# Two steps of the first batch set ahead of a filler, and the filler cut from 22 to 8 identity products

## The chip, the core and the metric

The kernel runs on one core of a Trainium2 chip. A core has a matrix engine (PE in the profile, with PEld for its weight loads), a vector engine (DVE), a scalar engine (ACT), GpSimd (POOL) and SyncE (SP), which here only issues DMAs. Every engine takes its instructions in the order in which they were written down for it, and waits on semaphores for what other engines or DMAs have to deliver. The metric is the time of one execution in microseconds (us) on the device; lower is better. Queries, keys, values and all products are 32-bit floats; the three weight matrices are given in 64 bits.

## What is computed

Retention in its parallel form (8 batches of 576 tokens, 8 heads of 64), followed by a gated feed-forward block on 4608 tokens of width 512, with 1536 hidden columns:

```python
scores = scale * np.matmul(q, k.transpose(0, 1, 3, 2))
gamma = 1.0 - 2.0 ** (-5.0 - np.arange(H, dtype=np.float32))
Dmat = np.where(rel >= 0, gamma[:, None, None] ** rel[None, :, :], 0.0)
attn_out = np.matmul(scores * Dmat[None], v)
x = np.ascontiguousarray(attn_out.transpose(0, 2, 1, 3)).reshape(B * S, H * D)
g = x @ w_gate
out = (g * (1.0 / (1.0 + np.exp(-g))) * (x @ w_val)) @ w_out
```

## The kernel before

**Retention.** Two heads make a pair; a batch has four pairs (0 to 3 in the first batch), and a sequence is cut into chunks of 64 tokens. For each pair the kernel makes transposed queries and keys, the scores of each chunk with itself (`scores`, L558), the sums of keys times values of each chunk (`new_states`, L528), their running, decayed sums over the chunks (`masked`: L565 masks the scores, L569 copies, L581 joins pairs of chunks, L588 runs over odd chunks, L593 fills the even ones), and two contributions to the output: that of the chunk itself (`own_values`, L517), and that of all past chunks, which multiplies the running sums by the queries (`earlier_values`, L544). Before the latter PE waits until the last product of `own_values` is complete. `to_x` (L625) copies the result to `xs`, the input of the feed-forward block.

**Feed-forward.** The first 512 tokens are handled chunk by chunk of the width (a chunk is a pair's 128 columns): `up0(f, chunks, parts)` multiplies the f-th block of 128 hidden columns, part 0 being the gate and part 1 the value weights, each into a bank of its own (bankA and bankB for even f, bankC and bankE for odd f). After the fourth chunk ACT takes the silu (L874) and DVE the product (L875). The other tokens follow in four tiles of 1024, in a scheme with fewer products than the plain one (L1204 and L1410), which fills the time from about 170 us on.

**Weights** arrive as 64-bit floating-point numbers and are rounded to 32 bits on the core before use. `split(j)` is two ACT instructions (L398, L399) that take a half of a loaded weight apart into two buffers, which alternate with j; `rounding(j)` is two DVE instructions (L415, L416) that put the rounded weight together. `split` may also issue the next weight's load, on SP's queue or, from the sixth weight on, on POOL's (L379, L381). SP's queue carries the loads of the pairs too (L269, L273, L279 in the first batch; L290 and L299 later). Pairs of the later batches have their queries and keys transposed by DVE (L477), which then waits for the DMA.

**Order.** The schedule is written out by hand: the order of calls in the function's body is the order on each engine. `pieces` is a list of postponed DVE and ACT work: `go_on(n)` issues the next n of them, and a piece that is itself a list (here L581; L588; L593) can be issued part by part with `part_on()`. The stretch that the change touches runs from about 16 to 22 us of the profile: pair 1's outputs, the first two weights, and the transposes of pair 3 (L466). In it stands a loop of 22 products of a 64x64 corner of the identity with itself into bankB (L1461), whose result nobody reads; PE does them while the first weight is being rounded.

Of the kernel before, what the change touches and what calls it, by code (L numbers as in the profile page):

```python
# [132 lines left out]
def kernel(  # L133
# [110 lines left out]
    def whole(i):  # L244

        return HP <= i < needed(2) - 2
# [136 lines left out]
    def bits_of(i, f):  # L383

        if i < NUP:
            return raws[i].rearrange("p c (f m two) -> p f c m two", f=2, two=2)[:, f]
        return raws[i].rearrange("p (f c) (d m two) -> p f (c d) m two", f=2, m=P, two=2)[:, f]

    def split(j):

        i, f = halves[j]
        bits = bits_of(i, f)
        top, ulp = [rest[:, part_at + 512 * (2 * n + j % 2) : part_at + 512 * (2 * n + j % 2 + 1)] for n in range(2)]
        blocks = lambda a: a.rearrange("p (c m) -> p c m", m=P)
        nc.scalar.activation(out=blocks(top), in_=bits[:, :, :, 1].bitcast(F32), func=AF.Prelu, scale=2.0 ** -112, alpha=2.0 ** 32)  # L398
        nc.scalar.activation(out=blocks(ulp.bitcast(I32)), in_=bits[:, :, :, 0].bitcast(U32), func=AF.Copy, scale=2.0 ** -29)  # L399
        parts[j] = top.bitcast(I32), ulp.bitcast(I32)  # L400
        m = j - 2 if 1 < j < 4 else j // 2
        if f and m != RAWS and m + RAWS + (m < RAWS) < len(order):
            if j == 3:
                held.append(lambda: load_w(m + RAWS + (m < RAWS)))
            else:
                load_w(m + RAWS + (m < RAWS))

    def rounding(j, ahead=True):

        i, f = halves[j]
        dst = weights[i][1][f].bitcast(I32)
        top, ulp = parts.pop(j)
        nc.vector.tensor_scalar(out=dst, in0=top, scalar1=3, scalar2=None, op0=ALU.logical_shift_left)  # L415
        nc.vector.tensor_tensor(out=dst, in0=dst, in1=ulp, op=ALU.add)  # L416
        if ahead and j + 1 < len(halves):
            split(j + 1)
# [23 lines left out]
    def places(i):  # L442
        return other if i < HP and i % 2 else (ret, ret_last, state)
# [56 lines left out]
    def value(i, hl, c):  # L500

        if whole(i):
            x = c // 2 % 2
            at = c % 2 + c // 4 * 2
        else:
            x, at = c % 2, c // 2
        return outer[half[hl ^ x], x, ts(at, L)]

    def own_values(i, n=0):

        s, ret = st[i], places(i)[0]
        cs = [a + d for a in (1 - n, 5 - n) for d in (0, 2)] if whole(i) else range(0 if n else NC - 1)
        for c in cs:
            for hl in range(2):
                rows, at = chunk(i, hl, c)
                start = n == 0 and c in (cs[:2] if whole(i) else (0, 1))
                m = nc.tensor.matmul(value(i, hl, c), s["v"][rows, at], ret[rows, c % 2 if whole(i) else hl, c // 2],  # L517
                                     start=start, stop=start, skip_group_check=True)
        if n == 0:
            s["own"] = m  # L520
# [10 lines left out]
    def earlier_values(i):  # L531
        s, (_, ret_last, state) = st[i], places(i)

        wait = nc.tensor.nop()
        tc.add_manual_dep(wait.ins, s["own"].ins.name,
                          mybir.DependencyInfo(mybir.DependencyClass.Sync, mybir.DependencyReason.DATA), reason="row halves")
        own_values(i, 1)
        for hl in range(0 if i < HP else 2):
            rows, at = chunk(i, hl, NC - 1)
            nc.tensor.matmul(xr[half[hl]], s["v"][rows, at], ret_last[rows],  # L540
                             start=False, stop=False, skip_group_check=True)
        for c in (1, 3, 4, 6, 5, 7, 2, 8) if whole(i) else range(1, NC - (i < HP)):
            for hl in range(2):
                nc.tensor.matmul(xr[half[hl]] if c + 1 == NC else value(i, hl, c), state[half[hl], c, :],  # L544
                                 s["qT"][half[hl], ts(c, L)], start=False, stop=True, skip_group_check=True)
# [52 lines left out]
    def to_x(i):  # L598
        b, p = divmod(i, HP)
        st.pop(i)  # L600

        def blocks(lo, end):
            for n in range(2):
                cs = [c for c in range(lo, end, 2) if c // 2 % 2 == n]
                if not cs:
                    continue
                at = dst(lo, end).rearrange("p (c r i) -> p c r i", r=2, i=L)[:, (cs[0] - lo) // 2 :: 2]
                src = outer[:, n, cs[0] // 4 * P : (cs[-1] // 4 + 1) * P].rearrange("p (c r i) -> p c r i", r=2, i=L)
                for rows, to in exchanged if n else straight:
                    if light(i):  # L610
                        nc.scalar.copy(out=at[to], in_=src[rows])
                    else:
                        decay = (qry_odd if n else qry)[rows, p].unsqueeze(1).unsqueeze(1)
                        nc.vector.tensor_tensor(out=at[to], in0=src[rows], in1=decay.to_broadcast(list(src[rows].shape)), op=ALU.mult)

        def chunks(lo, end):
            for r in range(2):
                cs = range(lo + (lo + r) % 2, end, 2)
                if not cs:
                    continue  # L620
                n = len(cs)
                for src, to in exchanged if r else straight:
                    table = (qry_odd if r else qry)[src, p]
                    if scaled(i):
                        nc.scalar.copy(out=dst(lo, end)[to].rearrange("p (c r i) -> p c r i", r=2, i=L)[:, :, r], in_=xo[src, :, r])  # L625
                        continue
                    at = dst(cs[0] - r, cs[0] - r + 2 * n) if cs[0] - r >= lo and cs[-1] + 2 - r <= end else None
                    if at is not None:
                        at = at[to].rearrange("p (c r i) -> p c r i", r=2, i=L)[:, :, r]
                        nc.vector.tensor_tensor(out=at, in0=xo[src, cs[0] // 2 : cs[0] // 2 + n, r],  # L630
                                                in1=table.unsqueeze(1).to_broadcast([at.shape[0], n, L]), op=ALU.mult)
                    else:
                        for c in cs:
                            nc.vector.tensor_tensor(out=dst(c, c + 1)[to], in0=xo[src, c // 2, r], in1=table, op=ALU.mult)

        def both():

            if i < HP:
                pass
            elif light(i):  # L640
                nc.scalar.copy(out=dst(NC - 1, NC), in_=xr)
            else:
                nc.vector.tensor_tensor(out=dst(NC - 1, NC), in0=xr, in1=qry[:, p], op=ALU.mult)
            lo = 0
            while lo < NC - 1:
                end = lo + 1
                while end < NC - 1 and where(end)[0] == where(lo)[0]:
                    end += 1
                if whole(i):
                    blocks(lo, end)  # L650
                else:
                    chunks(lo, end)
                lo = end

        def dst(lo, end):
            n, o = where(lo)
            return xs[n][:, p, o : o + (end - lo) * L]

        def where(c):

            n, o = divmod(b * S + c * L - starts[0], TW)
            return n, o - (TW - T0 if n == 0 else 0)

        return [both]
# [109 lines left out]
                             start=False, stop=True, skip_group_check=True)  # L774
        nc.scalar.copy(out=xs[0][:, 0], in_=outer[:, 0])

    def new_pair(i):
        scores(i, True)
        new_states(i)
        pieces.extend(masked(i))  # L780
        go_on(3)

    def turn_pair(i):
        for f in transposes(i):
# [54 lines left out]
    def go_on(n):  # L839
        for _ in range(min(n, len(pieces))):  # L840
            while part_on():
                pass

    def part_on():

        if pieces and isinstance(pieces[0], list):
            pieces[0].pop(0)()
            if pieces[0]:
                return True
            pieces.pop(0)  # L850
        elif pieces:
            pieces.pop(0)()
        return False
# [600 lines left out]
    split(0)  # L1454
    rounding(0, False)
    scale_run(3)
    new_pair(2)
    own_values(1)
    split(1)
    for _ in range(22):  # L1460
        nc.tensor.matmul(bankB[0:D, 0:D], ident[0:D, 0:D], ident[0:D, 0:D], start=True, stop=True)  # L1461
    up0(0, [0], [0])
    earlier_values(1)
    to_x(1)[0]()
    put = transposes(3)
    rounding(1, False)
    for f in put:
        f()
    up0(0, [1], [0])
    up0(0, [0], [1])  # L1470
# [161 lines left out]
```

## Time and profile before

| | |
|---|---|
| three runs | 1014.41 us median, 1012.95 to 1018.09 |
| the profiled execution | 1013.87 us |
| its span, first to last instruction | 1012.2 us |
| PE busy | 1005.7 us (99%) |
| DVE, POOL, ACT busy | 713.4, 571.9, 286.4 us |
| PE idle before 1.55 us | start of the first product |
| granted clock of PE | 1.00 |

Times in the profile count from the span's start. A line of a timeline gives the start, the duration from the first to the last instruction of the group, engine, source line, operation, the tile written and those read, the shape, and how often; in brackets stands the engine's idle time before it and what ended it. PE's 32-bit products appear as two records each, so 22 products are x44. A line of the chain of waits gives start, duration and what was being done or waited for. In rows by stretches, each engine has its busy time and its number of records; the last three columns are the granted clock, the share of the 16 DMA engines that was in use (transfers that overlap count each, so it can pass 1), and GB/s.

### The profile page before, as it was taken

The numbers are of one execution on the slowest core, as the hardware profiler recorded it, in microseconds if no ns is written. First come the engines' busy times: TensorE is split into PE (matmuls) and PEld (weight loads), VectorE is DVE, ScalarE is ACT, GpSimd is POOL, SyncE is SP. The second block draws the span as 40 slices with busy tenths as digits, with TensorE's granted clock in tenths as the row PEclk, the third lists the DMA queues.
The fourth block names the chain that finished last, engine by engine and source line by source line (L and its number), as shares of the span: only waits on it lengthen the run. The fifth ranks groups of instructions, "written<-read, shape, count | busy, mean of one in ns | idle before, by whom it ended". The sixth has DMA issues, their size and how long they took to land.

```text
span 1012.2 us, 21328 instructions
## 1 busy us (share of the span) xinstructions
PE 1005.7 (99%) x8338; PEld 829.4 (82%) x8338; DVE 713.4 (70%) x1203; ACT 286.4 (28%) x636; POOL 571.9 (57%) x603
## 2 busy tenths in 40 slices
PE   9999999999999999999999999999999999999998
PEld 7655555888888888888888888888888888888887
DVE  5567988677875766977777678866575767566645
ACT  4644622131423312133322202233320012233110
POOL 3510458979475228575565157746672586566514
PEclk9999999999999999999999999999999999999999
DMA  9999986888788887757668686434454554445553
GB/s 242 280 265 258 201 236 230 222 236 217 182 209 215 215 213 215 195 157 197 180 183 225 176 203 197 152 131 161 162 173 141 154 189 147 146 155 184 179 161 103
DMA packets 273932, 194.44 MB, mean 192 GB/s; under 512 B 212328, under 2 KB 241896, under 8 KB 273832
## 3 DMA queue, kind: packets, MB, share of 16 engines
q1 hardware_dynamic: 248296, 94.77, 38.6%
q10 hardware_dynamic: 21360, 84.29, 25.5%
q0 software_dynamic: 4176, 14.03, 4.3%
q8 instruction: 66, 1.08, 0.5%
q14 instruction: 34, 0.28, 0.1%
HBM read 154.11 MB, written 38.93 MB: 191 GB/s over the span
## 4 chain that ended last, share of the span: by engine, by line
PE 90%; SPq 3%; DVE 2%; DMA 2%; issue 1%; POOL 1%; ACT 1%; ACTq 0%; DVEq 0%; POOLq 0%
PE bankC L1204 11%; PE bankB L1204 11%; PE bankA L1204 11%; PE bankE L1204 11%; PE bankB L1410 7%; PE bankE L1410 7%; PE bankC L1410 7%; PE bankA L1410 6%; SPq L299 2%; PE inner L1204 2%; PE outer L1204 2%; PE outer L517 2%; PE outer L544 1%; PE inner L558 1%; PE inner L528 1%
## 5 line engine op out<-in xcount | busy, mean ns | idle before, releaser
L1060 POOL TENSOR_TENSOR rest<-rest 128x512 f32<-128x512 f32 (+1 forms) x139 | 147.8, 1075 | 159.9 <-DVE rest L1060 112.5
L1219 POOL TENSOR_TENSOR arena<-rest,io 128x256 f32<-128x256 f32 x168 | 123.5, 746 | 89.9 <-ACT io L1218 89.3
L1218 ACT ACTIVATE io<-rest 128x256 f32<-128x256 f32 x192 | 79.2, 417 | 200.8 <-DVE rest L1060 138.9
L1204 PE MATMUL bankB<-rest,arena 128*128 128x256 f32 x448 | 114.9, 380 | 0.1
L1060 DVE TENSOR_TENSOR rest<-bankB,rest 128x512 f32<-128x512 f32 x116 | 78.6, 686 | 41.8 <-PE bankB L1204 30.0
L1204 PE MATMUL bankC<-rest,arena 128*128 128x256 f32 x416 | 106.3, 380 | 0.0
L1204 PE MATMUL bankA<-rest,arena 128*128 128x256 f32 x412 | 104.8, 379 | 0.0
L1060 DVE TENSOR_TENSOR rest<-bankA,rest 128x512 f32<-128x512 f32 x111 | 75.3, 686 | 38.4 <-PE bankA L1204 19.2
L1060 DVE TENSOR_TENSOR rest<-bankC,rest 128x512 f32<-128x512 f32 x110 | 74.6, 685 | 37.6 <-PE bankC L1204 26.6
L1060 DVE TENSOR_TENSOR rest<-bankE,rest 128x512 f32<-128x512 f32 x106 | 71.9, 686 | 36.5 <-PE bankE L1204 21.4
L1204 PE MATMUL bankE<-rest,arena 128*128 128x256 f32 x372 | 94.9, 380 | 0.0
L1204 PEld LDWEIGHTS bankB<-rest,arena 128*128 128x128 f32 x448 | 84.5, 190 | 12.8 <-POOL arena L1060 0.7
L1204 PEld LDWEIGHTS bankC<-rest,arena 128*128 128x128 f32 x416 | 78.5, 190 | 11.4 <-DVE rest L1060 0.8
L1204 PEld LDWEIGHTS bankA<-rest,arena 128*128 128x128 f32 x412 | 78.1, 190 | 10.8
L1204 PEld LDWEIGHTS bankE<-rest,arena 128*128 128x128 f32 x372 | 70.3, 190 | 10.1 <-DVE rest L1060 0.6
L1060 POOL TENSOR_TENSOR arena<-arena 128x256 f32<-128x256 f32 (+1 forms) x76 | 70.4, 950 | 8.1 <-PE bankC L1204 6.7
L1410 PE MATMUL bankB<-arena 128*128 128x256 f32 x264 | 61.0, 381 | 0.0
L1410 PE MATMUL bankE<-arena 128*128 128x256 f32 x264 | 60.8, 380 | 0.0
L1410 PEld LDWEIGHTS bankE<-arena 128*128 128x128 f32 x264 | 50.0, 190 | 6.9
L1410 PEld LDWEIGHTS bankB<-arena 128*128 128x128 f32 x264 | 49.8, 190 | 6.9
L1410 PE MATMUL bankC<-arena 128*128 128x256 f32 x240 | 55.2, 379 | 0.0
L1410 PE MATMUL bankA<-arena 128*128 128x256 f32 x228 | 52.5, 380 | 0.0
(291 smaller groups left out, 1875.3 us busy)
## 6 DMA issues: line engine op xcount, KB each, us to landing
arena<-up ACTq DMA_DIRECT2D x63, 896.0 KB, 4.8
arena<-dn ACTq DMA_DIRECT2D x65, 384.0 KB, 3.1
arena<-dn SPq DMA_DIRECT2D x39, 384.0 KB, 3.1
out_dram<-rest SPq DMA_DIRECT2D x31, 256.0 KB, 4.5
qk<-in_q_dram SPq DMA_DIRECT2D x108, 72.0 KB, 4.4
qk<-in_k_dram SPq DMA_DIRECT2D x108, 72.0 KB, 3.3
dn<-rest SPq DMA_DIRECT2D x26, 256.0 KB, 3.6
up<-arena SPq DMA_DIRECT2D x13, 512.0 KB, 4.8
```

The costliest lines, as they stand in the source:

```text
L299: queue.dma_start(out=qk[a * SQ : (a + 1) * SQ, n], in_=src[b, 2 * p + a // 2, :, (a % 2) * SQ : (a % 2 + 1) * SQ].rearrange("(j t) d -> t ...
L517: m = nc.tensor.matmul(value(i, hl, c), s["v"][rows, at], ret[rows, c % 2 if whole(i) else hl, c // 2], start=start, stop=start, skip_grou ...
L528: nc.tensor.matmul(z[half[hl], r, c], s["kn"][chunk(i, hl, 2 * c + r)], s["v"][rows, at], start=True, stop=True, skip_group_check=True)
L544: nc.tensor.matmul(xr[half[hl]] if c + 1 == NC else value(i, hl, c), state[half[hl], c, :], s["qT"][half[hl], ts(c, L)], start=False, stop ...
L558: nc.tensor.matmul(sc[chunk(i, hl, 2 * c + r)[0], r if whole(i) else hl, c], kT[half[hl], at], qT[half[hl], at], start=True, stop=True, sk ...
L1060: eng.tensor_tensor(out=out, in0=a, in1=b, op=ALU.add if sign > 0 else ALU.subtract)
L1204: m = nc.tensor.matmul(b[:, g * TB : (g + 1) * TB], w[:, g], x, start=(opens and g == 0), stop=True, skip_group_check=True)
L1218: nc.scalar.activation(out=s, in_=src[:, 0:TB], func=AF.Silu)
L1219: (nc.vector if busy and o != 2 and qd + 1 < NQ else nc.gpsimd).tensor_tensor(out=hid[:, qd, 2 * H + h, 2 * T + t], in0=src[:, TB : 2 * TB ...
L1410: nc.tensor.matmul(b[:, m * TB : (m + 1) * TB], lhs[:, qd, ts(m, P)], w[:, qd], start=(opens and qd == 0 and m == 0), stop=(qd == NQ - 1), ...
```

## The change

In the first batch, between the scores of pair 2 and the transposes of pair 3:

- `new_pair(2)` issues two postponed pieces instead of three, and L581 of the third by itself; the rest of it (three L588 and L593, the running sums of pair 2) follows after the second weight's rounding.
- `earlier_values(1)` and `to_x(1)` of pair 1 stand ahead of the identity products and of the first product with a weight, instead of behind.
- `rounding(1)` stands ahead of L588 and L593 on DVE, instead of behind.
- The loop makes 8 identity products instead of 22.

What is computed stays the same. On SP and POOL, and on ACT, the order of instructions is unchanged; on PE the 14 products of L544 change places with the identity products and one L871; on DVE one L415 and one L416 change places with the running sums.

```diff
-    def new_pair(i):
+    def new_pair(i, n=3):
         scores(i, True)
         new_states(i)
         pieces.extend(masked(i))
-        go_on(3)
+        go_on(n)
...
     scale_run(3)
-    new_pair(2)
+    new_pair(2, 2)
+    part_on()
     own_values(1)
+    earlier_values(1)
     split(1)
-    for _ in range(22):
+    rounding(1, False)
+    go_on(1)
+    to_x(1)[0]()
+    for _ in range(8):
         nc.tensor.matmul(bankB[0:D, 0:D], ident[0:D, 0:D], ident[0:D, 0:D], start=True, stop=True)
     up0(0, [0], [0])
-    earlier_values(1)
-    to_x(1)[0]()
-    put = transposes(3)
-    rounding(1, False)
-    for f in put:
+    for f in transposes(3):
         f()
```

## The prediction

> **What bounds the kernel now.** I read the page first. PE is busy 1005.7 of 1012.2 us, and the list of PE's own waits over the whole span holds six entries. So the question is not what the edit saves, but whether PE can use it. The chain of waits shows the place of the edit:
>
> ```profile
> 16.05 0.47 PE outer L517 x32
> 16.52 2.51 PE bankB L1461 x44
> 19.03 1.06 PE bankA L871 x2
> 20.09 0.61 PE outer L544 x28
> 20.70 0.59 PE bankC L466 x4
> ```
>
> The 22 identity products (L1461, two records each) are 44 records in 2.51 us, that is 57 ns a record and 114 ns a product. They stand in the chain because PE's order is fixed, while PE's next real work, L871, needs the first rounded weight: that is DVE's L416 at 17.47 + 0.69 = 18.16, 0.8 us before L871 starts. So at least some of the filler is not needed. The list of PE's waits is the second view:
>
> ```profile
> PE bankB L732 <- POOL ident masks.py:199: 1.6, 1, 1.6
> PE bankA L871 <- ACT io L874: 0.4, 1, 0.4
> PE inner L747 <- DVE kT L741: 0.3, 1, 0.3
> PE bankA L871 <- ACT rest L625: 0.2, 1, 0.2
> ```
>
> The second entry decides my forecast: PE waits once more, 80 us after the edit. Timelines of PE, ACT and DVE around it, in this order:
>
> ```profile
> 102.36 3.70 PE L871 MATMUL bankA<-rest,arena 128*128 128x512 f32 x8 [0.38 <-ACT io L874]
> 98.11 0.68 ACT L398 ACTIVATE rest<-rest 128x512 f32<-128x512 f32 x1 [7.61 <-issue]
> 101.73 0.57 ACT L874 ACTIVATE io<-bankA 128x512 f32<-128x512 f32 x1
> 96.03 0.78 DVE L477 STREAM_TRANSPOSE kT<-qk 128x576 f32<-128x576 f32 x1 [3.45 <-DMA qk<-in_k_dram]
> 97.60 0.43 DVE L415 TENSOR_SCALAR arena<-rest 128x512 int32<-128x512 int32 x1
> ```
>
> Read from the bottom: DVE stands 3.45 us before its transposition L477 until a key block has landed at 96.03. Behind it in DVE's queue is the rounding L415 (to 98.03). ACT's next split L398 needs the buffer that L415 reads, and starts at 98.11 after 7.61 us of idleness. Three splits stand ahead of the silu L874, which frees PE's bank at 102.30. So at 102.36 PE is held by a DMA landing, with 0.38 us to spare. Last, the DMA by stretches (the last two columns are DMA share and GB/s):
>
> ```profile
> 20.00:62.00 42.00, 41.53 (x393) 25.18 (x393) 22.19 (x46) 23.05 (x45) 18.63 (x30) 1.00 1.15 282
> 62.00:102.00 40.00, 39.98 (x400) 20.04 (x398) 32.77 (x72) 22.73 (x41) 5.30 (x7) 1.00 1.02 256
> 102.00:1012.00 910.00, 906.06 (x7236) 768.38 (x7236) 648.20 (x1065) 232.21 (x535) 540.39 (x550) 1.00 0.65 185
> ```
>
> From 20 to 102 us the transfers fill the DMA engines (share 1.15 and 1.02); afterwards 0.65, and PE waits no more.
>
> **The change, part by part.** The sum goes against the profiled execution: 1013.87 us, span 1012.2, so 1.67 around it; the median of the three runs, 1014.41, lies 0.54 above.
>
> *PE up to 22 us.* Removed: 14 products x 0.114 = 1.60 us; the eight left take 0.91. Moved: L544 of pair 1 (0.61) now follows L517, ending at 16.52. It also needs the states of L593 (15.48 + 0.48 = 15.96, done) and L517's completion, which cost 0.09 us at the next such place (24.53 to 24.62): start 16.61, end 17.22, products until 18.13. L871 then waits for L416 (18.16); the shortest releases seen cost 0.05, so 18.21, end 19.27. Next are pair 3's transposes L466. Their key blocks were issued at about 14.7 and 15.2; blocks of L273 landed 3.5 to 4.1 us after issue, the query blocks of L269 5.5, so the second is there between 18.7 and 20.7. I take 19.5, near the key row: PE waits 0.2 to 0.3, L466 starts at 19.55 (20.63 before). The scaled queries (POOL's L720, 18.79 + 1.04 = 19.83) are there for the second four at 20.04. Then L871's second chunk needs ACT's three L625 (1.13): ACT is free at 18.58 + 0.66 = 19.24, L544 ended at 17.22, so 20.37, and PE comes at 20.64. Before: 21.93, with a wait of 0.21 that now goes. **Lead: 21.93 - 20.64 = 1.3 us.** With the late bound of the keys it is 0.1, with the early one 1.5.
>
> *DVE.* The second rounding (L415, L416; 20.86 to 22.11 = 1.25) goes ahead of three L588 and L593 (19.18 to 20.95 = 1.77). Its splits are done at 19.24, so it ends at 19.15 + 1.25 = 20.4; its reader, L871 into bankB, comes at 22.89 - 1.3 = 21.6. The states now end at 22.2; their reader L544 of pair 2 comes at 24.62 - 1.3 = 23.3. So this move costs nothing while 1.1 us of cover is left; if rounding came later than that, PE would lose the excess. Nothing else on DVE is overtaken.
>
> *ACT, POOL, SP.* Their orders are unchanged; instructions only come earlier. The fourth split (L398 at 26.39) needs a weight piece issued at about 19.9; such a piece took 5.4, so 25.3: ACT gains 1.0 instead of 1.3. Its rounding then ends at 27.3 (28.36), before bankE's L871 at 27.9. So PE keeps its 1.3 beyond 30 us. No DMA is added or reordered within a queue. SP's weight load at 24.15 waits for an L399 and comes earlier by up to 1.3, but two loads of 1 MB, issued at 20.48 and 21.02, are in flight; POOL's at 27.94 and 35.18 come 1.0 to 1.3 earlier.
>
> *From 30 to 102 us.* PE has no wait in between, and its suppliers there have margins above a microsecond or move with it. At 102.36 the silu still hangs on the landing at 96.03. From 24.15 on SP issues loads back to back, each as room becomes free, and the engines are full, so I leave 96.03 where it is: the wait grows from 0.38 to 1.68 us and takes back the whole 1.3. Bounds: -1.3 if the landing moves along, +1.3 by the second rival below. I take zero, since DVE's stall of 3.45 is wider than any lead.
>
> Sum: 1013.87 - 1.3 + 1.3 = 1013.9; beside the median, **1014.4 us**.
>
> **A rule beside a row.** PE's transposes of 128x128 take 0.85 us for four at 5.09 (bankE) and 0.45 for four at 6.77 (bankC) in the chain, after steady work since 1.55; the granted clock reads 1.00 throughout. PE starts at half pace and doubles after some 5 us. The Trainium skill, "TensorE: Matmul & The Clock Gate", Part 1, says that the clock is halved until some 3.4 us of sustained work, and halved again after an idle window of that length. The trace agrees with the doubling; none of its idle stretches after 7 us is long enough to show the rest. By that rule the removed filler could cost the pace, and an estimate from the page would be 3.4 us at half rate, 1.7 us lost.
>
> **The rivals.**
> *The lead survives.* If the key blocks land 1.3 us earlier, or PE isn't held at 102 in typical executions, the gain stays: 1014.4 - 1.3 = 1013.1. For it: the margin is only 0.38, and DMA dips to share 0.93 between 15 and 20 us. Against: the share of 1.15 afterwards.
> *Earlier weight loads push the keys back (slower).* POOL's loads are released by ACT, hence by PE. Up to 1.3 us earlier, they use engines that SP's key blocks use. At 282 GB/s, half to POOL, 1 to 1.3 us are 140 to 180 KB, so keys land 0.5 to 0.65 later; if it repeats for the next pair, 1.3. PE then waits longer at 102: +0.5 to +1.3, so 1014.9 to 1015.7, say 1015.2. It decides as soon as the landing moves later at all, because the lead has made PE the waiting side. Against: what POOL takes early it doesn't take later. The Trainium skill, "DMA: Bandwidth & Descriptors", on queues, rings and completion order, has each engine take turns between its queues; this speaks for this case, and no row here shows the turns.
> *PE drops to half pace near 19 us (slower).* At half pace for the 5 us that the start took, PE loses 2.6; less the lead of 1.3 and the margin of 0.38, +0.9: 1015.3. Against: the new idle pieces sum to some 0.4 us, and the present kernel had 0.29 and 0.21 without a change of pace.
> *The change does nothing of what it says:* excluded, the order of instructions on PE and DVE shows both moves.
>
> **How the numbers follow.** Chances: held at 102, no change, 0.60; lead survives 0.18; keys pushed back 0.15; half pace 0.03; something that I don't see 0.04. The runs of before spread from 1012.95 to 1018.09, so medians wobble by about a microsecond. The range takes in 1013.1 and 1015.7 and 0.9 on either side: 1012.2 to 1016.6. A measurement tells about 0.5%, 5 us, from no change. No case has a price near it; only the unseen one could: faster 0.02, same 0.95, slower 0.03.
>
> **What would show it.** Right: L871's second chunk at about 20.6; PE's wait at 102 about 1.7, with L477's landing within 0.5 of 96.0; everything behind shifted by less than 0.5. Lead surviving: that landing near 95, the wait still below 0.5. Keys pushed back: landing after 96.5. Half pace: L871's records doubled around 20 us. Wrong in the first step: L466 waiting beyond 20.2, or L544 of pair 2 waiting for L593.

## The result, and the profile after

The changed kernel takes 1019.83 us (median of 7 runs, 1017.31 to 1022.43) where the kernel before takes 1014.00 (7 runs beside it): a ratio of 1.0050, 95% interval 1.0036 to 1.0065. It is slower by half a per cent, and the interval lies clear of 1. In a second series it was 1017.73 against 1014.02, ratio 1.0035 (1.0016 to 1.0053). The prediction said no change. The profiled execution took 1019.12 us, with a span of 1017.4, 5.2 us longer than before.

Around the edit nearly all of it came as written down. Timeline of PE and DVE of the changed kernel (start, duration, engine, line, operation, tile, shape, count; in brackets idle time and what ended it):

```profile
19.70 0.63 PE L466 MATMUL bankC<-ident,rest 128*128 128x128 f32 x4 [0.19 <-DMA rest<-in_k_dram]
20.61 1.02 PE L871 MATMUL bankA<-rest,arena 128*128 128x512 f32 x2
21.47 1.02 PE L871 MATMUL bankB<-rest,arena 128*128 128x512 f32 x2
23.29 0.68 PE L544 MATMUL outer<-rest,state 64*64 64x64 f32 x28 [0.18 <-PE outer L517]
28.33 1.98 PE L871 MATMUL bankE<-rest,arena 128*128 128x512 f32 x4 [0.29 <-DVE arena L416]
31.73 1.12 PE L871 MATMUL bankA<-rest,arena 128*128 128x512 f32 x2
...
19.21 1.03 DVE L415 TENSOR_SCALAR arena<-rest 128x512 int32<-128x512 int32 x1
20.38 0.69 DVE L416 CUSTOM_DVE_ANT_0 arena<-arena,rest 128x1024 uint16<-128x1024 uint16 x1
```

The second chunk starts at 20.61 (21.93 before): the lead of 1.3 us is there. At 31.73 it has shrunk to 0.77 (32.50 before), because the fourth rounding came later than I had it. Four entries from the list of PE's waits then show what the lead became:

```profile
PE bankA L871 <- ACT io L874: 3.1, 1, 3.1
PE bankA L1204 <- DMA arena<-up: 1.0, 1, 1.0
PE bankE L871 <- DVE arena L416: 0.3, 1, 0.3
PE bankC L1204 <- DMA arena<-up: 0.2, 1, 0.2
```

The first one is eight times the wait that I had looked at, and it is not at 102 us but at 70. Timeline of the changed kernel there:

```profile
67.32 0.78 DVE L477 STREAM_TRANSPOSE kT<-qk 128x576 f32<-128x576 f32 x1 [9.42 <-DMA qk<-in_k_dram]
68.67 0.38 DVE L415 TENSOR_SCALAR arena<-rest 128x512 int32<-128x512 int32 x1
69.14 0.70 ACT L398 ACTIVATE rest<-rest 128x512 f32<-128x512 f32 x1 [12.85 <-DVE arena L415]
72.72 0.58 ACT L874 ACTIVATE io<-bankA 128x512 f32<-128x512 f32 x1
73.35 5.40 PE L871 MATMUL bankA<-rest,arena 128*128 128x512 f32 x8 [3.08 <-ACT io L874]
78.58 3.60 PE L871 MATMUL bankB<-rest,arena 128*128 128x512 f32 x8
```

It is the chain that the prediction drew for 102 us, one key block of a pair earlier: DVE stands until the key block has landed (67.3), its rounding stands behind that, ACT's splits behind the rounding, the silu behind the splits, and PE behind the silu. The same places in the kernel before:

```profile
62.34 0.78 DVE L477 STREAM_TRANSPOSE kT<-qk 128x576 f32<-128x576 f32 x1 [3.67 <-DMA qk<-in_k_dram]
67.77 0.59 ACT L874 ACTIVATE io<-bankA 128x512 f32<-128x512 f32 x1
70.98 3.70 PE L871 MATMUL bankA<-rest,arena 128*128 128x512 f32 x8
```

There the silu was done 2.6 us before PE came (68.36 to 70.98). The block now lands 5.0 us later, and PE comes 0.7 us earlier. The eight records of L871 behind the wait take 5.40 instead of 3.70 us. The rows by stretches of the changed kernel say why (the third column from the right is the granted clock):

```profile
70.00:73.30 3.30, 0.28 (x18) 0.14 (x10) 2.87 (x6) 3.30 (x7) 0.70 (x1) 1.00 0.70 92
73.30:77.00 3.70, 3.65 (x5) 1.57 (x6) 3.50 (x6) 3.61 (x8) 0.77 (x1) 0.54 0.89 277
```

A mean clock of 0.54 over 3.7 us is half rate for 3.4 us: 1.70 us lost, directly behind an idleness of 3.08 us. The Trainium skill, "TensorE: Matmul & The Clock Gate", Part 1, describes this: a free-running window of 3413 ns, and half rate after an idle one. The trace agrees on the length: the granted clock reads half for 3.41 us, from 73.47 on.

So the balance of the profiled executions is: wait 3.08, half clock 1.70, less 0.71 of lead, gives 4.07 at the next bank (78.58 against 74.51). The old wait of 0.38 at 102 us has gone, and another 0.3 is recovered in places that I can't name: 3.37 at L1204's wait for L1249, which both have (277.85 against 274.48). Two waits of L1204 for loads, 1.04 at 432 us and 0.22 at 480, add 1.26. The remaining 0.6 us can't be put down to a wait.

### The profile page after: what moved, and what is told of

The parts are those of the page before. It is cut to its first block, busy times and chain, and to the rows that moved or that the text cites. A ratio compares the mean times of both kernels' runs of the same rounds, so it can differ in the third digit from the quotient of the medians.

```text
span 1017.4 us, 21275 instructions
## 1 busy us (share of the span) xinstructions
PE 1005.5 (99%) x8310; PEld 828.4 (81%) x8310; DVE 714.3 (70%) x1203; ACT 286.0 (28%) x636; POOL 571.5 (56%) x603
## 4 chain that ended last, share of the span: by engine, by line
PE 71%; DMA 2%; SPq 0%; DVE 0%; ACT 0%; issue 0%
PE bankC L1204 10%; PE bankB L1204 9%; PE bankA L1204 9%; PE bankE L1204 9%; PE bankB L1410 7%; PE bankE L1410 7%; PE bankC L1410 7%; PE bankA L1410 6%; PE outer L1204 2%; PE inner L1204 2%; DMA arena<-up 1%; PE outer L517 1%; PE outer L544 1%; PE inner L558 1%; PE inner L528 1%; SPq L299 0%
## 5 line engine op out<-in xcount | busy, mean ns | idle before, releaser
L1204 PE MATMUL bankB<-rest,arena 128*128 128x256 f32 x448 | 114.5, 380 | 0.0
L1204 PE MATMUL bankC<-rest,arena 128*128 128x256 f32 x416 | 106.3, 380 | 0.2 <-DMA arena<-up 0.2
L1204 PE MATMUL bankA<-rest,arena 128*128 128x256 f32 x412 | 104.8, 379 | 1.0 <-DMA arena<-up 1.0
L1204 PE MATMUL bankE<-rest,arena 128*128 128x256 f32 x372 | 94.9, 380 | 0.0
L1204 PEld LDWEIGHTS bankB<-rest,arena 128*128 128x128 f32 x448 | 84.8, 190 | 11.7
L1204 PEld LDWEIGHTS bankC<-rest,arena 128*128 128x128 f32 x416 | 78.5, 190 | 11.8 <-DVE rest L1060 0.6
L1204 PEld LDWEIGHTS bankA<-rest,arena 128*128 128x128 f32 x412 | 78.1, 190 | 12.1 <-DVE rest L1060 1.4
L1204 PEld LDWEIGHTS bankE<-rest,arena 128*128 128x128 f32 x372 | 70.3, 190 | 10.1 <-DVE rest L1060 0.6
```

Of the source, the lines that this page charges most:

```text
L1204: m = nc.tensor.matmul(b[:, g * TB : (g + 1) * TB], w[:, g], x, start=(opens and g == 0), stop=True, skip_group_check=True)
```

## The experiments

Two things had to be explained: why a key block lands later although no DMA was moved, and why the lead is not merely taken back but turned into a loss.

One measure is used throughout. A run's granted clock is listed as a mean over the span to three digits; one stretch of 3.4 us at half rate is 0.0017 of it, so 0.998 stands for one such stretch. "Half clock" in the table counts the runs with 0.998 or less.

### Parts of the edit, each alone

```diff
 e1, kernel before:   for _ in range(22)  ->  for _ in range(8)
 e2, changed kernel:  for _ in range(8)   ->  for _ in range(22)
 e3, kernel before, only DVE's move:
-    new_pair(2)
+    new_pair(2, 2)
+    part_on()
     own_values(1)
     split(1)
+    rounding(1, False)
+    go_on(1)
...
-    rounding(1, False)
 e4, kernel before, only PE's move:
     own_values(1)
+    earlier_values(1)
     split(1)
+    to_x(1)[0]()
...
-    earlier_values(1)
-    to_x(1)[0]()
```

> The kernel before with 8 instead of 22 identity products and nothing moved. PE can start the first weight product at about 18.2 us (its rounding ends at 18.16) instead of 19.03, so it keeps a lead of some 0.8 us at 22 us; DVE's order is the old one. Theory A (PE's lead lets ACT release the later weight loads earlier, and these push the key block of pair 5 back): that block lands near 67 instead of 62.3 us, PE waits 2 to 3 us at about 70 us, 1017 to 1020 us. Theory B (the rounding that DVE now does ahead of the running sums is the cause): the block lands near 62.3, 1013 to 1014.5 us. Theory C (the order of the transfers tips over with any shift of a few tenths, whatever its sign or place): somewhere between 1012 and 1020, in no relation to the lead.

> The changed kernel with 22 identity products again: both moves, no lead (the second chunk of the first weight at about 21.9 us, as before). Theory A: 1013.5 to 1015 us, key block of pair 5 near 62.3. Theory B: 1018 to 1020, as the changed kernel. Theory C: anywhere from 1012 to 1020.

> The kernel before with the second rounding ahead of the running sums on DVE alone; PE's order and the 22 products as before. No lead for PE at 22 us; ACT's fourth split is bound by its weight's landing. Theory A: 1013.5 to 1015. Theory B: 1018 to 1020, key block near 67. Theory C: anywhere from 1012 to 1020.

> The kernel before with the values of past chunks of pair 1 and their copy ahead of the 22 identity products; DVE's order as before. PE's sum of work up to the transposes is unchanged, so the lead is 0 to -0.1 us; the first weight product comes 0.7 us later. Theories A and B: 1013.5 to 1015. Theory C: anywhere from 1012 to 1020.

With 22 products all are as before: e2 1014.15, e3 1013.99, e4 1013.47 us, against 1013.68; ratios 1.0004, 1.0001 and 1.0000, all intervals within 0.9985 to 1.0021. With 8 products and nothing moved, e1 takes 1016.61 (ratio 1.0023, 0.9994 to 1.0052: its interval just includes 1). So both moves are harmless, and it is the cut from 22 to 8 products that seems to do the damage: B falls. A fits by its sign only, since e1 stays below its 1017 us, with a block at 65.9 and a wait of 1.39 us. And one expectation was wrong: with no lead the key block was to land near 62.3. Timeline of e3:

```profile
66.03 0.78 DVE L477 STREAM_TRANSPOSE kT<-qk 128x576 f32<-128x576 f32 x1 [7.21 <-DMA qk<-in_k_dram]
72.11 3.70 PE L871 MATMUL bankA<-rest,arena 128*128 128x512 f32 x8 [0.93 <-ACT io L874]
```

It landed at 66.0, PE waited 0.93 us, and the run still took 1014.42. The one profile of the kernel before, on which I had built, was an early case. So theory C stays possible for the landing, though the times of e2 to e4 speak against it. The lateness here is also of its own kind: a load raises its semaphore 16 times, and of this block's last load 15 increments were there at 62.69, the last one only at 66.00 (in e4 62.50 and 65.93). In the changed kernel 15 were there at 67.24 and the last at 67.30.

### Same landing, more idleness? Products late in the kernel

Theory T said that the block lands where it always does, and that PE only idles longer and loses its clock. Then it helps to use up the lead at any place before the wait.

```diff
 e5, changed kernel, unaltered
 e8, changed kernel:  for _ in range(8)  ->  for _ in range(15)
 e6 (n = 6), e7 (n = 14), ahead of up0(6), the product that waits near 70 us:
+        for _ in range(n):
+            nc.tensor.matmul(outer[:, 1, 384:512], ident, ident, start=False, stop=True, ...)
 e9 (n = 6), e10 (n = 14), the same products ahead of end_scores() (L688)
 e12 (n = 6), the same products ahead of the loop over f, at 39 us
 e11 (n = 6), ahead of up0(1, range(2)), at 26 us:
+    for _ in range(6):
+        nc.tensor.matmul(bankC[:, 0:P], ident, ident, start=True, stop=True)
```

> The changed kernel again, unaltered, for a second profile beside the experiments. Theory R (the lead before 34 us shifts the releases of the weight loads, and with them the key block of pair 5, to a later landing): the block lands at 66.6 to 68 again, against 62.3 to 66.0 in the four profiles without the full lead. Theory T (the landings are the same, 62 to 66; PE comes to the wait near 70 us earlier, idles for longer, and past some 2 to 3 us of idleness the granted clock is halved for 3.4 us, 1.7 us lost): the block lands between 62 and 66.5, and what is lost beyond it is the half clock. Both: about 1019.5 us.

> The changed kernel with 6 products of the whole identity (128x128, about 0.22 us each, 1.3 us in all) on PE directly ahead of the product that waits near 70 us for the silu. Everything before is as in the changed kernel; PE's lead is used up at that place, so that its idleness there is 1.3 us shorter, 1.8 instead of 3.1 us. Both theories: no half clock any more, 1.000 in nearly all runs, as after the idle 1.5 and 1.6 us of an earlier run. Theory R: the late landing stays, 1017 to 1018 us. Theory T: 1013.5 to 1015 us.

> As the run before with 14 products, about 3.1 us: PE hardly idles at that place. Theory R: 1017 to 1018 us, no half clock. Theory T: 1014 to 1016 us (in executions whose key block lands early the products themselves delay PE by up to 1.5 us).

> The changed kernel with 15 instead of 8 identity products: half the lead, 0.5 to 0.7 us at 22 us instead of 1.3. Theory R: about half the loss, 1016 to 1018 us, the block landing between 65.5 and 67. Theory T: the clock is halved in fewer of the runs, some in ten; 1014 to 1016.5 us.

e6 and e7 missed their aim. The products write a bank that DVE still had to read, so they waited themselves. Timeline of PE in e6:

```profile
82.42 2.93 PE L1519 MATMUL outer<-ident 128*128 128x128 f32 x12 [12.12 <-DVE rest L693]
```

They took 1028.96 and 1030.37 us. All they show is that 12 us of idleness cost more than 12 us: the clock was 0.992 or 0.993 in all eight runs, some 13.7 us at half rate. e5 is the second series given above (1017.73). Its profile has the block at 65.95, a wait of 2.35 us at 72 without half clock, and one of 3.55 at 106 us with it. e8, with 15 products, took 1017.30 (ratio 1.0021, 1.0007 to 1.0035), no less than e1 with 8. The next four put the products where they wait for nothing:

> The changed kernel with 6 products of the whole identity (1.3 us) ahead of the small products L688 that precede the wait near 70 us; they wait for nothing. PE's lead is used up only there, so all releases up to 68 us stay early. Theory R (the early releases make pair 5's key block land later): the landing stays near 66.5 us (65.9 to 67.3 in four profiles with the full lead, 62.3 to 66.0 in three without), PE still idles about 1.3 us beyond what the kernel before does, no half clock: 1015 to 1017 us. Theory T (landings unaffected; the loss is idleness past the length at which the clock is halved): 1013.5 to 1014.7 us, 1.000 in nearly all runs.

> As the run before with 14 products (3.1 us): PE hardly idles there. Theory R: 1015 to 1017 us. Theory T: 1014 to 1016 us, since where the block lands early the products themselves hold PE up by as much as 1.8 us. Both: no half clock near 73 us.

> The changed kernel with 6 products of the whole identity into bankC ahead of that bank's first products at 26 us: the lead is used up there, before the weight loads that ACT releases at 27.6 and 34.9 us in the kernel before. Theories R and T: 1013.5 to 1015 us; if the harm were done before 26 us (the weight loads and key blocks of pair 3), 1017 us or more.

> The changed kernel with 6 products of the whole identity at 39 us, behind the first batch's last products with the first weights: the weight load released at 34.4 us (35.2 before) stays early, all later work of PE is back in the old place. Theory R: 1015 to 1017 us, landing near 66.5. Theory T: 1013.5 to 1014.7 us.

Against 1014.40 for the kernel before: e9 1016.98, e10 1015.98, e11 1018.85, e12 1018.22 us. T falls by e9, e11 and e12: with most of the lead used up at 68, 26 or 39 us, the time did not come back. (e10 comes to 1.6 us above the kernel before, its ratio 1.0018 with 1.0001 to 1.0034, which both theories allowed.) R does not fit either, since e11 gives up most of the lead at 26 us, before the weight loads that the kernel before issues at 27.94 and 35.18, and is one of the slowest; and in e12 the block was there at 63.63. For e11 there had been a third forecast, harm done before 26 us, and its 1018.85 fits that, but e11 and e12 had a second trouble, shown below. What does hold is the part of the clock. Timeline of PE in e10:

```profile
69.21 3.39 PE L804 MATMUL outer<-ident 128*128 128x128 f32 x28
73.40 3.70 PE L873 MATMUL bankA<-rest,arena 128*128 128x512 f32 x8 [0.41 <-ACT io L876]
```

PE was released at 73.40, as in the changed kernel (73.35), but had been kept busy, and the eight records behind the wait took 3.70 instead of 5.40 us. One of its 10 runs had the half clock, against 6 of 7 and 5 of 10 of the changed kernel. The whole run is shorter by 3.7 us (span 1013.7 against 1017.4).

In e12 PE was stopped by something else. Timeline of PE:

```profile
71.15 0.44 PE L688 MATMUL outer<-rest 64*64 64x64 f32 x12
76.11 0.48 PE L688 MATMUL outer<-rest 64*64 64x64 f32 x3 [4.52 <-issue]
```

Between two products that wait for no semaphore PE stood still for 4.52 us. e11 has 2.17 us at the same place, e8 0.91. At 73.37 the DMA records of e12 have a packet of 16384 bytes on queue 8, which the profile lists as `instruction`. That PE had run out of code is read from two agreements. In e8, e11, e12 and x3 (below) PE went on 1.4 to 1.7 us after the end of such a packet. And the stall stands at a place in the code: with 8 products fewer ahead of it, 3, 3 and 2 records before the end of L688 (e11, e12, x3), and with 7 fewer, so with two records more ahead, 5 before the end (e8).

### Where PE's code is fetched

PE's code comes during the execution, in packets of 16 KB on queue 8. The row of this queue in the kernel before from 40 to 46 us, and in the changed kernel from 46 to 52 (packets, MB, share of the 16 engines):

```profile
q8 instruction: 1, 0.02, 1.7%
```

```profile
q8 instruction: 1, 0.02, 1.2%
```

The packet starts at 43.3 us before, and at 50.2 in the changed kernel; the next one at 64.8 and 69.5. A cut of 14 products takes 28 records of products and 28 of weight loads out of PE's stream, so that everything behind stands 56 instructions earlier in the code. By the Trainium skill, "Runtime: NRT & Kernel Launch", "Instruction fetch mechanics", a block of 16 KiB holds 256 instructions. The trace agrees: the kernel before has 66 such packets, and its 8338 records of products and 8338 of weight loads are 65.1 times 256.

What such a packet does to other transfers is seen in the counts of the semaphores, which a load raises 16 times. In the kernel before a code packet starts at 13.12 and takes 1.19 us. A weight piece issued at 10.62 has 15 of its 16 increments at 14.88, the last at 16.11. In the changed kernel a packet starts at 50.20 and takes 1.18 us. A small key load of POOL issued at 48.77 has 15 at 52.97, the last at 54.82; the same load in the kernel before, with no code packet near, 51.36 and 51.40. So one share in 16 comes late, and whoever waits for the load waits for the last share. It is the same with all POOL loads issued from 47.14 to 48.77, last increments 1.9 to 2.1 us behind the 15th, and POOL issues the next weight load (L381) at 54.47 instead of 50.29, just when the load issued at 47.68 has landed. Over all 20 profiles, among the loads of SP and POOL issued from 10 to 110 us whose increments can be told apart, the last one is a microsecond or more behind the 15th in 124 of 386 that had a code packet under way between issue and 15th increment, and in 46 of 450 that had none. So code packets go with late shares, but late shares come without them too.

This packet can't be the whole cause. The last load of the key block is issued at 55.62 in the changed kernel and at 51.99 in the kernel before, so 3.6 of the 5.0 us are there before it is on its way. But SP's queue is 2.9 us late at 43.92 already (40.99 before), ahead of the packet at 50.20; and e3, which loses nothing, is as late at that place (44.11).

In most of the slow kernels so far lead and place of the code had changed together. Four runs take them apart, two more mend what these left open:

```diff
 x1, changed kernel, and x4, kernel before: 22 products of 24 columns
+    for _ in range(22):
+        nc.tensor.matmul(bankB[0:D, 0:24], ident[0:D, 0:D], ident[0:D, 0:24], start=True, stop=True)
 x2, changed kernel: 8 products, 7 of them of 192 columns (no lead, 14 fewer)
 x3, kernel before: 14 products, 8 of them of 128 columns (no lead, 8 fewer)
 x5, changed kernel, at 39 us:
+    for _ in range(14):
+        nc.tensor.matmul(outer[:, 1, 384:392], ident, ident[:, 0:8], start=False, stop=True, ...)
 x6, both moves, 22 products, a lead made elsewhere (up0):
+                n = P if f == 0 and c == 1 else T0
+                last_up[0] = nc.tensor.matmul(bank[:, 0:n], w, xs[0][:, c, 0:n], ...)
```

> The changed kernel with 22 identity products of 24 instead of 64 columns: by length about 22 x 0.043 = 0.94 us, so nearly the whole lead of 1.3 us, with the old number of PE instructions. Theory L (the lead is what costs): 1017 to 1020 us, the clock halved in half of the runs. Theory P (the place of PE's code fetches is what costs): the code packet starts at about 65 us as in the kernel before, 1013.5 to 1014.7 us.

> The changed kernel with 8 identity products, 7 of them of 192 columns: 2.4 to 2.6 us, no lead, but the new number of PE instructions. Theory L: 1013.5 to 1014.7 us. Theory P: 1017 to 1020 us.

> The kernel before with 14 identity products, 8 of them of 128 columns: as long as the 22, no lead, nothing moved, but 8 PE products fewer. Theory L: 1013.5 to 1014.7 us. Theory P: the fetch falls into the small products near 70 us, as in the two runs with 8 products fewer that stalled 2.2 and 4.5 us there; 1015 to 1018 us.

> The kernel before with 22 identity products of 24 columns and nothing moved: the lead of the run with 8 products (0.4 to 0.6 us at 22 us) with the old number of PE instructions. Theory L: 1016 to 1017 us, as that run (1016.6). Theory P: 1013.5 to 1014.7 us.

> The changed kernel with 14 products of the whole identity with 8 columns at 39 us, behind the last products with the first weights: the lead (0.8 to 1.3 us) stands until 39 us and is then used up (14 products at 0.11 to 0.12 us), and the number of PE instructions ahead of what follows is the old one again. Theory P (the place of the code fetch costs): the code packet starts at 42 to 45 us and the next near 65, as in the kernel before; 1013.5 to 1015 us. Theory L (the early lead costs): as the run with 6 products at 39 us, 1018 us.

> Both moves, 22 identity products as before, and PE's lead made in another way: two products of the first hidden block, the second chunk into bankA and into bankB, compute 128 of their 512 columns (384 columns of two sums are left out). That saves 0.65 us at 21.5 and another 0.65 at 24 us, so from there on the lead is that of the changed kernel, 1.3 us, with the old number of PE instructions. Theory P: no loss, 1012.5 to 1014.7 us (a gain only as far as no key block holds PE). Theory L: 1017 to 1020 us.

In the table the lead is taken at the first product into bankC: how much earlier it starts, counted from L517 of pair 1, than the 11.55 us of the kernel before. "Key block" is the start of L477 on pair 5's keys.

| run | PE products before 70 us | lead | key block | PE idle near 71 us | median (before) | ratio, interval | half clock |
|---|---|---|---|---|---|---|---|
| e2 | as before | 0.3 | 63.80 | 0 | 1014.15 (1013.68) | 1.0004, 0.9986 to 1.0021 | 2 of 10 |
| e3 | as before | -0.1 | 66.03 | 0.9 | 1013.99 (1013.68) | 1.0001, 0.9987 to 1.0015 | 1 of 10 |
| e4 | as before | 0.4 | 65.96 | 1.5 | 1013.47 (1013.68) | 1.0000, 0.9985 to 1.0015 | 1 of 10 |
| x4 | as before | 0.0 | 62.61 | 0 | 1014.91 (1014.74) | 0.9991, 0.9975 to 1.0007 | 4 of 10 |
| x1 | as before | -1.3 | 60.20 | 0 | 1015.82 (1014.74) | 1.0003, 0.9984 to 1.0022 | 7 of 10 |
| x5 | as before from 39 us | 1.6 to 39 us | 63.64 | 0 | 1015.88 (1014.07) | 1.0024, 1.0010 to 1.0037 | 3 of 10 |
| x6 | as before | 1.5 | 67.17 | 3.2 | 1017.05 (1014.07) | 1.0018, 0.9996 to 1.0039 | 7 of 10 |
| x3 | 8 fewer | 0.1 | 67.05 | 2.0 | 1017.89 (1014.74) | 1.0022, 1.0003 to 1.0040 | 6 of 10 |
| x2 | 14 fewer | 0.5 | 67.41 | 2.9 | 1018.36 (1014.74) | 1.0019, 1.0002 to 1.0035 | 6 of 10 |
| e1 | 14 fewer | 0.7 | 65.93 | 1.4 | 1016.61 (1013.68) | 1.0023, 0.9994 to 1.0052 | 5 of 10 |
| after | 14 fewer | 1.6 | 67.32 | 3.1 | 1019.83 (1014.00) | 1.0050, 1.0036 to 1.0065 | 6 of 7 |

For e9 to e12 and e8, which the table leaves out, the block starts at 66.47, 67.35, 66.78, 63.63 and 68.49.

x1 and x4 had no lead after all: 22 products of 24 columns took as long as 22 of 64. Timeline of PE and row by stretches of x1:

```profile
17.49 2.60 PE L1466 MATMUL bankB<-ident 64*64 64x24 f32 x42
...
20.00:23.60 3.60, 3.60 (x13) 2.44 (x12) 2.24 (x6) 1.22 (x3) 0.68 (x2) 0.53 0.95 260
```

42 records in 2.60 us are about 60 ns each. And although PE never paused, the clock was halved between 20 and 23.6 us, so that x1 even came late. Both stand in the table as runs without a lead.

x2 and x3 decide the first point. They have little lead or none (0.5 and 0.1 us); x3 has the old order on every engine, and x2 differs from e2, whose lead is 0.3, by nothing but fewer and longer products. They lose 3.6 and 3.2 us by the medians, 1.9 and 2.2 by the ratios, and both intervals lie above 1, though by little (1.0002 and 1.0003). The others point the same way: with 7, 8 or 14 products fewer ahead of 68 us (the changed kernel, e1, e5, e8 to e12, x2, x3) the medians are 1.6 to 5.8 us above the kernel before; with 22 products and a lead below 0.5 us (e2, e3, e4, x1, x4) they are from 0.2 below to 1.1 above. Timeline of x2:

```profile
67.41 0.78 DVE L477 STREAM_TRANSPOSE kT<-qk 128x576 f32<-128x576 f32 x1 [9.23 <-DMA qk<-in_k_dram]
73.44 5.40 PE L871 MATMUL bankA<-rest,arena 128*128 128x512 f32 x8 [2.90 <-ACT io L874]
```

These are the changed kernel's lines, without its lead. In x3 the block was as late, and part of PE's time went into the stall for code. Timelines of DVE and PE of x3:

```profile
67.05 0.78 DVE L477 STREAM_TRANSPOSE kT<-qk 128x576 f32<-128x576 f32 x1 [6.92 <-DMA qk<-in_k_dram]
72.38 0.27 PE L688 MATMUL outer<-rest 64*64 64x64 f32 x2 [1.54 <-issue]
```

x6, which leaves 384 columns of two sums out, is the other half: a lead of 1.5 us and the old number of instructions, code packets at 42.9 and 63.4 us. Timeline of x6:

```profile
67.17 0.78 DVE L477 STREAM_TRANSPOSE kT<-qk 128x576 f32<-128x576 f32 x1 [9.58 <-DMA qk<-in_k_dram]
73.20 5.40 PE L872 MATMUL bankA<-rest,arena 128*128 128x512 f32 x8 [3.24 <-ACT io L875]
```

By the median it loses 3.0 us, with the half clock in 7 of 10 runs; the interval of its ratio just includes 1. x5, whose lead ends at 39 us and whose code has the old number of products ahead of it from there, loses 1.8 us. It is not a clean test: its packets came at 45.9 and 67.8 us, later than in the kernel before, and its profile has the half clock at 41 us, behind its own 8-column products, though its seven runs without half clock still have a median of 1015.46. So that the lead costs something by itself is likely, and not shown. By the medians either of the two brings much of the loss, and together they are not twice as bad (3.7 and 5.8 us in two series).

A last trace of the code's place is at 432 us, where the changed kernel waits 1.04 us for a load of L1017. Of the ten profiles with 7, 8 or 14 PE products fewer at that point, eight have this wait (0.2 to 1.7 us); of the ten with the old number none has it. Timeline of PE of the changed kernel:

```profile
432.25 1.10 PE L1204 MATMUL bankA<-rest,arena 128*128 128x256 f32 x4 [1.04 <-DMA arena<-up]
```

A code packet starts at 424.5 there, and at 418.9 in the kernel before.

**What is shown and what is not.** Shown: the moves are harmless; fewer PE products, with the filler as long as before, cost 2 to 3.6 us (x2 and x3, lower ends of the intervals just above 1); in the profiles of the changed kernel, x2, x3, x6, e8 and e12 the time is lost in the chain from the key block's landing to the silu, in a stall for code beside it, or in both; idlenesses of 2.9 us or more there cost another 1.7 us or more by the clock. (e9, at 1017.77, shows no such wait: its 3.4 us of idleness are four waits of 0.64 to 1.06 us elsewhere.) Shown as going together, and followed in single transfers: a code packet and one share of a load that comes 1.2 to 2.1 us late. Left open: how the new place of the code becomes 3 to 5 us of a key block, and whether and how the lead by itself (x6) delays it too. The transfers are issued in a closed loop (landing, rounding, split, next weight load, and POOL and SP wait for earlier landings), and I can show only that small shifts at its start leave it in another order. None of the kernels of the 18 runs was measurably faster than the kernel before.

## Why the prediction was wrong

- **PE up to 22 us: right.** L871's second chunk at 20.61 (20.64 predicted), L466 at 19.70 with a wait of 0.19 for its keys (19.55 and 0.2 to 0.3).
- **DVE: right, with a term mis-sized.** L415 took 1.03 us instead of 0.42, so the second rounding ended at 21.07, not 20.4. Its reader came at 21.47, so the cover held, with 0.4 us left instead of 1.2. L544 of pair 2 came at 23.29 (23.3) and waited only for L517.
- **ACT's gain of 1.0 us at the fourth split: wrong.** The weight piece landed at 26.24, not 25.3; the split started at 26.31, the rounding ended at 28.27, and PE waited for it. The lead at 32 us was 0.77, not 1.3. The piece had been issued at 20.40 (19.9 assumed) and took 5.8 us (5.4).
- **"PE has no wait in between, and its suppliers there have margins above a microsecond": this is the step that failed.** The margin of the silu at 71 us was 2.6 us in the profile of before, but it hung on a landing, and I treated landings as fixed. The block landed at 62.3 in that profile; in the others with the old code and no lead it was there from before 60.2 to 66.0. A margin read from one execution was not a margin. In the changed kernel the block came at 67.3, and in place of no wait there stood one of 3.08 us and then 1.70 us of half clock.
- **"I leave 96.03 where it is": wrong.** The block of pair 7 landed at 98.4. PE has no wait there in the profile: it ran 4.07 us late since 78 us.
- **The rival with the keys pushed back** had the right sign and the right chain, at 0.15, but at +0.5 to +1.3 us it was too small, and its cause (POOL's loads 1.0 to 1.3 us earlier) was there only in part: they came 0.08 and 0.76 us earlier. Its sign, a landing after 96.5, came true.
- **The rival with the half clock** was looked for at 19 us, with a price of 2.6 us (half of 5 us is 2.5). It came at 73 us, with 1.70. The estimate of 1.7 us for one stretch at half rate was right in size.
- **Not thought of at all:** that taking PE instructions out moves the code fetches of all that follows. Range and chances had no term for it beyond the 0.04 for something unseen.

## What to carry to other kernels

Where the DMA engines are full and a silu, a rounding or a transposition hangs on a landing, a lead on PE may not be worth its microseconds: ask which landing it will run into, and take the spread of that landing from several profiles. Filler products that nobody reads may have two uses that a timeline doesn't show: they can keep the clock up (as the 14 products of e10 seem to have done), and their instructions set the place of every later code fetch. So take them out by shortening or lengthening products as well as by counting them, and compare before reading anything into a loss of 0.3%.

## What the runs showed of the hardware

- Code fetches are not free. The Trainium skill ("Runtime: NRT & Kernel Launch", "Instruction fetch mechanics") calls the crossing of a 16 KiB boundary mostly hidden. Here PE stopped at it for 0.91, 1.54, 2.17 and 4.52 us (e8, x3, e11, e12), always among the small products L688 near 71 us.
- Small products have a floor. A record of 64 or of 24 columns took about 60 ns, so 24 columns gained nothing. The Trainium skill, "TensorE: Matmul & The Clock Gate", Part 1, gives some 62 ns per matmul instruction where the array's work is shorter, with the hardware decode off. The trace agrees with the time per record; which way of decoding was on, no run here shows.
- The clock was halved after idlenesses of 2.86, 2.90, 3.08, 3.24, 3.55 and 4.52 us (e8, with 0.91 just ahead of it, x2, the changed kernel, x6, e5, e12), not after 2.35, 2.17 and 1.63 (e5, e11, e4). The Trainium skill, "TensorE: Matmul & The Clock Gate", Part 1, speaks of an idle window of about 3.4 us; a somewhat shorter pause was enough here. And it was halved with no pause at all behind 2.6 us of 24-column products (x1), and again behind the 8-column products of x5 at 41 us.
- 131 runs of the kernel before, taken beside these, have a median of 1014.27 us. 17 of them have the half clock; their median is 1017.73, that of the others 1014.12. So a part of what looked like noise in this kernel comes with the event that the change made frequent.
